# One decode step of attention beside a gated feed-forward: the first K tile's score products split around V's

## The chip, the cores and the metric

The kernel runs on one core of one Trainium2 chip. The metric is device time in microseconds of one execution; the kernel before took 2516.11 us, the median of 3 runs (2516.02 to 2516.18). The core has TensorE (PE, matrix products into the PSUM memory), VectorE (DVE), ScalarE (ACT), GpSimd (POOL) and SyncE (SP, which issues the transfers here). The engines run side by side and are tied to one another by semaphores.

## The reference

One token `x` of 512 values goes through two branches, and a gate mixes their outputs. Branch a is attention with 32 heads of 128 values against a cache of 65,536 keys and values for each head; branch b is a small gated feed-forward.

```python
q = (x @ wq).reshape(B, Sq, H, Dh).transpose(0, 2, 1, 3)
scores = einsum("bhqd,bhkd->bhqk", q, k_cache) * (Dh ** -0.5)
p = softmax(scores, axis=-1)
o = einsum("bhqk,bhkd->bhqd", p, v_cache)
a = o.transpose(0, 2, 1, 3).reshape(B, Sq, H * Dh) @ wo
b = (silu(x @ w_gate) * (x @ w_up)) @ w_down
g = sigmoid((x * gate_w).sum(-1, keepdims=True))
return g * a + (1 - g) * b
```

All inputs are bf16. The two caches are 537 MB each, nearly all of the 1087.65 MB that the kernel reads.

## The kernel before

*Tiles and buffers.* The keys of one head are cut into 4 tiles of 16,384 rows, which lie as 128 partitions x 128 keys x 128 values, and two tiles make a pair of 8.39 MB. There are 64 pairs (M), numbered m, two for each head. Two K buffers take the pairs in turn, and one V buffer holds a pair of V. They fill nearly all of the on-chip memory.

*Steps.* The first two pairs are handled in `prologue`. Then every engine runs steps m = 2, 3, ...: step m computes the scores of K pair m and applies the softmax weights of the head before to V pair m - 2. The 60 steps m = 2 to 61 are loops on VectorE, ScalarE and TensorE, with two steps to a round on TensorE; the last two are written out in `vector_end` and `tensor_end`. A head's first step is called b = 0 and its second b = 1 (`second` on TensorE).

*Scores.* VectorE multiplies a K tile by the query, repeated along the keys (`product`, L279), and then halves the 128 values by adding (L291, L309). Of the first tile of a pair only one halving is done (`add_once`, to 64 values, `WIDE`), then TensorE adds up the 64 in 16 products with the unit matrix into the bank `S_ps[0]`, 4 values each (`scores`, L513): the wide score products. The second tile is halved three times, the last time into `T_sb` with 16 values (`WIDTH`), and TensorE adds these in 4 narrow products into `S_ps[1]`. In either bank 4 values a key are left, which VectorE adds into `S_sb` (`fold`, L320). After a head's fourth tile VectorE takes the maximum (`row_max`, L326), which goes over ScalarE (`diag`) and TensorE (`max_turn`, L530) to `top_of` in the next step.

*V.* ScalarE turns a head's scores into weights `P_sb` (L417), half a head a step. TensorE then runs 64 products on V's pair (`values`, L537), each with 4 keys a partition as weights against 512 columns.

*Order on the engines.* Each engine runs its instructions in the order written. On TensorE a step has: in b = 1 the totals of the weights (`total`, L533); the 16 wide products; in b = 0 the wait for `P_sb`; the wait for V; V's 64 products; in b = 0 `total`; the query's spread for a later head (`query_spread`, L527); the 4 narrow products; the output's turn (`head_turn`, L545); `max_turn`. On VectorE: `product` of the first tile, `add_once`, `top_of` (b = 0) or the fold of the tile before (b = 1), `product` of the second tile, in b = 1 the three small instructions of `weight`, two sums, the fold of the first tile, the last sum into `T_sb`, and in b = 1 the second tile's fold and `row_max`.

*Loads.* SP issues all large loads into one queue, in the order V pair m - 1, K pair m + 2 (`sync_step`). The V load waits until V pair m - 2 is used up (`pe_V`, at the end of V's 64 products). The K load waits for the first narrow product of step m (`pe_K`), ahead of which every read of that K buffer stands. In `sync_end` the last tiles come singly, in halves or in smaller pieces, and then the output weights `wo`.

*Signals.* `take` waits for a credit and uses it up: `c_S[0]` comes from `add_once`, `c_S[1]` from the sum into `T_sb`, `c_P` from the weights, `c_V` from V's landing (through POOL), `c_q`, `c_o` and `c_m` from ScalarE. `fold` waits for `pe_S`, which the last of a tile's score products raises.

Of the kernel before, what the change touches and what calls it, by code (L numbers as in the profile page):

```python
# [11 lines left out]
NB = 128  # L12
PAIR = 2 * NB
QUAD = 4


WIDE = 64
WIDTH = 16

TURNED = 8  # L20
WO_CUTS = (0, 4, 8, 12, 16, 20, 24, 28, 30, 31, 32)
# [19 lines left out]
def kernel(  # L41
# [36 lines left out]
    def sb(name, shape, dtype=f32):  # L78
        return consts.tile(shape, dtype, name=name)
# [7 lines left out]

    T_sb = sb("T_sb", [P, NB, WIDTH], bf16)
    S_sb = [sb(f"S{i}_sb", [P, NBH]) for i in range(2)]
# [4 lines left out]
    ident_b, ones_b, q_diag = (sb(n, [P, P], bf16) for n in ("ident_b", "ones_b", "q_diag"))  # L94
# [16 lines left out]
    S_ps = [psum.tile([P, NB, QUAD], f32, name=f"S{i}_ps") for i in range(2)]  # L111
# [14 lines left out]
    def halves(buf):  # L126
        return [buf[:, i * NB * Dh : (i + 1) * NB * Dh].rearrange("p (j d) -> p j d", d=Dh) for i in range(2)]

    K_half, V_half = [halves(b) for b in K_bufs], halves(V_buf)
# [3 lines left out]
    def v_view(n):  # L133
        return {N - 4: K_half[0][1], N - 3: V_half[0], N - 2: V_half[1], N - 1: K_half[1][1]}[n]

    sync, act, dve, pool, pe = nc.sync, nc.scalar, nc.vector, nc.gpsimd, nc.tensor
# [3 lines left out]
    po, pe_x, pe_S, pe_V, pe_q, pe_m, pe_t, pe_o = (  # L140
        Events(nc, n) for n in ("po", "pe_x", "pe_S", "pe_V", "pe_q", "pe_m", "pe_t", "pe_o")
    )
# [24 lines left out]
    def wait(engine, events, value):  # L167
        key = id(engine), id(events)
        value -= taken.get(key, 0)
        if seen.get(key, 0) < value:  # L170
            engine.wait_ge(events.sem, value)
            seen[key] = value
# [88 lines left out]
    def product(n, start=0, stop=NB):  # L261
        K = K_half[n // 2 % 2][n % 2][:, start:stop, :]
        q = q_sb[n // G % 2]
        q_rep = bass.AP(tensor=q.tensor, offset=q[:, :].offset, ap=[list(q[:, :].ap[0]), [0, stop - start], [1, Dh]])
        m = n // 2

        if m == 0:
            wait(dve, (ka_in, kb_in)[n], 16)
        elif m == 1:
            wait(dve, kc_in, 16)  # L270
        elif n == N - 1:
            wait(dve, kb_in, 32)
        else:
            wait(dve, k_in[m % 2], 16 * (m // 2))
        if n < G:
            wait(dve, ac, marks["q"])
        else:
            wait(dve, ac_q, n // G)
        return own[0](dve.tensor_tensor(out=K, in0=K, in1=q_rep, op=ALU.mult))  # L279

    def add_halves(n, width, last, out=None, ahead=None):
        K = K_half[n // 2 % 2][n % 2]
        half, mark = Dh // 2, last
        while half >= width:
            wait(dve, own[0], mark)
            to = K[:, :, 0:half]
            if half == width and ahead is not None:
                fold(ahead)
            if half == width and out is not None:
                to = out  # L290
            ins = dve.tensor_tensor(out=to, in0=K[:, :, 0:half], in1=K[:, :, half : 2 * half], op=ALU.add)  # L291
            if half == width and out is not None:
                ins.then_inc(c_S[n % 2], 1)
            else:
                mark = own[0](ins)
            half //= 2
        marks["K", n] = mark
# [8 lines left out]
    def add_once(n, last):  # L306
        wait(dve, own[0], last)
        K, half = K_half[n // 2 % 2][n % 2], Dh // 2
        dve.tensor_tensor(  # L309
            out=K[:, :, 0:half], in0=K[:, :, 0:half], in1=K[:, :, half:], op=ALU.add  # L310
        ).then_inc(c_S[0], 1)


    def fold(n):
        h, g = divmod(n, G)
        if n < G or n >= N - G:
            wait(dve, pe_D, n + 1 if n < G else n + 1 - N + 2 * G)
        else:
            wait(dve, pe_S, n + 1 - G)
        return own[0](dve.tensor_reduce(  # L320
            out=S_sb[h % 2][:, g * NB : (g + 1) * NB], in_=S_ps[n % 2], axis=AXIS.X, op=ALU.add
        ))

    def row_max(h, folded):
        wait(dve, own[0], folded)
        (dv_max if h else dv_first)(dve.tensor_reduce(out=m_sb[:, 0:1], in_=S_sb[h % 2], axis=AXIS.X, op=ALU.max))  # L326

    def top_of(h):
        wait(dve, pe_m, 2 * h + 2)
        dv_top(dve.tensor_reduce(out=top[:, 0:1], in_=mT, axis=AXIS.X, op=ALU.max))  # L330

    def weight(h, t):
        wait(dve, pe_t, t)
        if h < H - 1:
            wait(dve, own[0], own[0](dve.tensor_reduce(out=tsum[:, 0:1], in_=tot, axis=AXIS.X, op=ALU.add)))
            total = tsum[:, 0:1]
        else:
            total = tot[:, 0:1]
        wait(dve, own[0], own[0](dve.reciprocal(recip[:, 0:1], total)))  # L339
        dv_rg(dve.tensor_tensor(out=rg[:, h % 2 : h % 2 + 1], in0=recip[:, 0:1], in1=gval, op=ALU.mult))  # L340

    def vector_step(m):
        h, b = divmod(m, MH)
        width, to = (WIDTH, T_sb) if m < M - 2 else (WIDE, None)
        last = product(2 * m)
        if to is not None:
            add_once(2 * m, last)
        if b == 0:
            top_of(h - 1)
        else:  # L350
            fold(2 * m - 1)
        if to is None:
            add_halves(2 * m, width, last)
        last = product(2 * m + 1)
        if b == 1:
            weight(h - 1, m - 1)
        add_halves(2 * m + 1, width, last, to, 2 * m)
        if b == 1:
            row_max(h, fold(2 * m + 1))

# [13 lines left out]
    def vector_round():  # L374
        own[0] = dv_loop
        for m in range(2, 2 + 2 * MH):
            vector_step(m)
        take_round(dve, dv_loop, vector_waits)
        own[0] = dv

    def vector_end():
        took_rounds(dve, vector_waits, (M - 4) // (2 * MH))
        vector_step(M - 2)
        vector_step(M - 1)
        top_of(H - 1)
        weight(H - 1, M - 1)
        wait(dve, pe_x, 5)
        out_a(dve.tensor_copy(out=out_sb[:, :HD], in_=a_ps[0]))
# [118 lines left out]
    def take(credit):  # L507
        pe.wait_ge(credit, 1)
        pe.sem_inc(credit, -1)  # L509

    def scores(n, src, width, events, start=0, stop=NB):
        for c in range(0, width, QUAD):
            ins = pe.matmul(  # L513
                S_ps[n % 2][:, start:stop, :], lhsT=ident_b, rhs=src[:, start:stop, c : c + QUAD],
                start=(c == 0), stop=(c == width - QUAD),
            )
            if c == 0 and events is pe_S and n == 1:
                pe_K(ins)
        if stop == NB:
            events(ins)  # L520

    def scores_direct(n, start=0, stop=NB):
        wait(pe, dv, marks["K", n])
        scores(n, K_half[n // 2 % 2][n % 2], WIDE, pe_D, start, stop)

    def query_spread(events):
        events(pe.matmul(qb, lhsT=ones_b, rhs=q_diag, start=True, stop=True))  # L527

    def max_turn(n=1):
        pe.matmul(mT, lhsT=ones_f, rhs=diag, start=True, stop=True).then_inc(pe_m.sem, n)  # L530

    def total(n=2):
        pe_t(pe.matmul(tot[:, :n], lhsT=ones_f, rhs=rs[:, :n], start=True, stop=True))  # L533

    def values(probs, view, start, stop, opens, closes):
        for j in range(start, stop, 4):
            ins = pe.matmul(  # L537
                O_ps, lhsT=probs[:, j : j + 4], rhs=view[:, j : j + 4, :],
                start=(opens and j == start), stop=(closes and j == stop - 4),
            )  # L540
        return ins

    def head_turn(opens=True):
        for c in range(4):
            ins = pe.matmul(  # L545
                oh, lhsT=O_sb[:, c * Dh : (c + 1) * Dh], rhs=ident_f[0:4, c : c + 1],
                start=(opens and c == 0), stop=(c == 3),
            )
        pe_o(ins)
# [133 lines left out]
    def tensor_step(m):  # L683
        second = m % MH
        if second:
            take(c_P)
            total()
        take(c_S[0])
        scores(0, K_half[m % 2][0], WIDE, pe_S)
        if not second:  # L690
            take(c_P)
        take(c_V)
        for i in range(2):
            pe_V(values(P_sb[:, i * NB :], V_half[i], 0, NB, i == 0, i == 1))
        if not second:
            total()
        take(c_q)
        query_spread(pe_q)
        take(c_S[1])
        scores(1, T_sb, WIDTH, pe_S)  # L700
        take(c_o)
        head_turn()
        take(c_m)
        max_turn()
# [115 lines left out]
```

## Time and profile before

| | us |
|---|---|
| unprofiled, median of 3 | 2516.11 |
| profiled execution, whole time | 2517.2 |
| its span | 2515.4 |
| VectorE busy in it | 2003.4 |
| TensorE busy (with modelled ends) | 1487.4 |
| ScalarE busy | 182.3 |

The three instructions of the loop that matter most: `product` of a tile is 8.7 us on VectorE (mean 8620 ns over 129, of which two are half tiles), a V product 379 ns from start to modelled end, a wide or tail score product 527 ns likewise. Matmuls overlap one another, so for their pace the spacing of their weight loads is read and not their duration.

How to read the lines below: a line of the timeline has its start, its length, the engine, the line of the kernel, the operation and out<-in, how many instructions were merged into it, and in brackets how long the engine stood idle before it and what ended that. SPq is SP issuing a load, PEld is TensorE loading weights. "PEclk" is the clock that TensorE was granted, as a share of full speed. The DMA share is the mean over the 16 transfer engines; in short windows it and the GB/s scatter, since a packet is counted where it ends.

### The profile page before, as it was taken

How to read it: one execution, taken by the hardware profiler on the slowest of the kernel's cores; microseconds unless marked ns; L12 is line 12 of the kernel's file. 1: busy time of each engine (PE TensorE's matmuls, PEld its weight loads, DVE VectorE, ACT ScalarE, POOL GpSimd, SP SyncE). 2: the span in 40 equal slices, each digit the busy share in tenths (PEclk: the TensorE clock that was granted, in tenths of full speed). 3: DMA queues.
4: the chain of work that ended last, by engine and by line, in shares of the span. 5: the costliest groups of instructions: out<-in, count | busy, mean ns of one | idle time of the engine just before them, and what ended most of it. 6: DMA issues, size and time to landing. Idle time of an engine off the chain costs nothing. (4 is left out here: it accounts for less than half of the span.)

```text
span 2515.4 us, 15705 instructions
## 1 busy us (share of the span) xinstructions
PE 1487.4 (59%) x6589; PEld 616.2 (24%) x6589; DVE 2003.4 (80%) x678; ACT 182.3 (7%) x503; POOL 0.7 (0%) x6
## 2 busy tenths in 40 slices
PE   2655655646556556465575565654745656547569
PEld 1322222222222222222222222222212222222223
DVE  5887887877878878779788788787787887977881
ACT  0000000000000000000000000000000000000000
POOL 0000000000000000000000000000000000000000
PEclk8777878778778777787787777877877778778789
DMA  9999999999999999999999999999999999999999
GB/s 414 438 433 436 435 434 434 434 434 434 435 434 434 434 434 434 435 436 435 435 435 434 437 434 435 435 434 437 435 434 434 434 434 434 434 435 434 434 431 387
DMA packets 22605, 1087.80 MB, mean 432 GB/s; under 512 B 2753, under 2 KB 3266, under 8 KB 4546
## 3 DMA queue, kind: packets, MB, share of 16 engines
q1 hardware_dynamic: 22306, 1087.65, 99.9%
q8 instruction: 7, 0.11, 0.0%
q10 hardware_dynamic: 288, 0.00, 0.0%
q14 instruction: 4, 0.03, 0.0%
HBM read 1087.64 MB, written 0.00 MB: 432 GB/s over the span
## 5 line engine op out<-in xcount | busy, mean ns | idle before, releaser
L279 DVE TENSOR_TENSOR K_buf<-K_buf,q_sb 128x16384 bf16<-128x16384 bf16 (+1 forms) x129 | 1112.0, 8620 | 348.8 <-DMA K_buf<-in_A_k_cache_dram 346.1
L513 PE MATMUL S_ps<-K_buf,ident_b 128*128 128x512 bf16 (+1 forms) x1104 | 388.9, 527 | 867.3 <-PEq L509 834.3
L537 PE MATMUL O_ps<-V_buf,P_sb 128*4 128x512 bf16 x3968 | 866.9, 379 | 28.6 <-PEq L509 28.3
L537 PEld LDWEIGHTS O_ps<-V_buf,P_sb 128*4 128x4 bf16 x3968 | 332.9, 85 | 560.1 <-issue 57.6
L291 DVE TENSOR_TENSOR K_buf<-K_buf 128x4096 bf16<-128x4096 bf16 (+1 forms) x127 | 433.7, 3415 | 3.1
L513 PEld LDWEIGHTS S_ps<-K_buf,ident_b 128*128 128x128 bf16 x1104 | 133.5, 126 | 1101.0 <-issue 1036.8
L309 DVE TENSOR_TENSOR K_buf<-K_buf 128x8192 bf16<-128x8192 bf16 x60 | 265.5, 4425 | 2.0
L392 ACT ACTIVATE O_sb<-O_ps 4x512 f32<-4x512 f32 x63 | 63.3, 1005 | 1705.1 <-PE qm_ps L527 1674.8
L320 DVE TENSOR_REDUCE S_sb<-S_ps 128x128 f32<-128x512 f32 x128 | 88.2, 689 | 105.4 <-PE S_ps L513 103.3
L530 PE MATMUL qm_ps<-diag,ones_f 128*128 128x128 f32 x126 | 33.5, 353 | 72.3 <-PEq L509 70.2
L545 PE MATMUL oh_ps<-ident_f,O_sb 4*128 4x1 f32 x504 | 64.3, 244 | 19.6 <-PEq L509 19.6
L291 DVE TENSOR_TENSOR T_sb<-K_buf 128x2048 bf16<-128x2048 bf16 x60 | 72.9, 1214 | 0.0
L545 PEld LDWEIGHTS oh_ps<-ident_f,O_sb 4*128 4x128 f32 x504 | 60.7, 186 | 49.7 <-issue 49.7
L513 PE MATMUL S_ps<-T_sb,ident_b 128*128 128x512 bf16 x240 | 64.7, 391 | 0.0
L530 PEld LDWEIGHTS qm_ps<-diag,ones_f 128*128 128x128 f32 x126 | 21.6, 215 | 76.3 <-issue 76.3
L392 ACT ACTIVATE bias<-top 128x1 f32<-128x1 f32 x32 | 6.5, 203 | 436.4 <-DVE top L330 436.4
L533 PE MATMUL tot_ps<-rs,ones_f 128*128 128x2 f32 (+1 forms) x126 | 24.8, 266 | 17.6 <-PEq L509 17.5
L392 ACT ACTIVATE oT<-whole_o,rg 32x1 f32 (+1 forms) x115 | 33.8, 294 | 4.7
L417 ACT ACTIVATE P_sb<-S_sb,bias 128x256 bf16<-128x256 f32 x62 | 31.5, 508 | 1.0
L533 PEld LDWEIGHTS tot_ps<-rs,ones_f 128*128 128x128 f32 x126 | 20.3, 202 | 36.5 <-issue 36.5
L513 PEld LDWEIGHTS S_ps<-T_sb,ident_b 128*128 128x128 bf16 x240 | 20.7, 96 | 15.9
L326 DVE TENSOR_REDUCE m<-S_sb 128x1 f32<-128x512 f32 x32 | 22.0, 686 | 1.1
(62 smaller groups left out, 197.1 us busy)
## 6 DMA issues: line engine op xcount, KB each, us to landing
K_buf<-in_A_k_cache_dram SPq DMA_DIRECT2D x4, 4096.0 KB, 32.9
V_buf<-in_A_v_cache_dram SPq DMA_DIRECT2D x2, 4096.0 KB, 21.3
V_buf<-in_A_v_cache_dram SPq DMA_DIRECT2D x4, 2048.0 KB, 17.6
V_buf<-in_A_wq_dram SPq DMA_DIRECT2D x1, 4096.0 KB, 12.3
K_buf<-in_A_v_cache_dram SPq DMA_DIRECT2D x1, 4096.0 KB, 29.9
K_buf<-in_A_wo_dram SPq DMA_DIRECT2D x7, 512.0 KB, 16.8
K_buf<-in_A_v_cache_dram SPq DMA_DIRECT2D x3, 1024.0 KB, 23.5
V_buf<-in_B_w_gate_dram SPq DMA_DIRECT2D x1, 1792.0 KB, 54.4
```

Source lines behind the costliest of these rows:

```text
L279: return own[0](dve.tensor_tensor(out=K, in0=K, in1=q_rep, op=ALU.mult))
L291: ins = dve.tensor_tensor(out=to, in0=K[:, :, 0:half], in1=K[:, :, half : 2 * half], op=ALU.add)
L309: dve.tensor_tensor(out=K[:, :, 0:half], in0=K[:, :, 0:half], in1=K[:, :, half:], op=ALU.add).then_inc(c_S[0], 1)
L320: return own[0](dve.tensor_reduce(out=S_sb[h % 2][:, g * NB : (g + 1) * NB], in_=S_ps[n % 2], axis=AXIS.X, op=ALU.add))
L326: (dv_max if h else dv_first)(dve.tensor_reduce(out=m_sb[:, 0:1], in_=S_sb[h % 2], axis=AXIS.X, op=ALU.max))
L392: return act.activation(out=out, in_=in_, func=ACT.Copy, scale=scale)
L417: return act.activation(out=out, in_=S_sb[h % 2][:, b * PAIR : b * PAIR + count], func=ACT.Exp, bias=bias[:, 0:1], scale=scale, accum_out= ...
L513: ins = pe.matmul(S_ps[n % 2][:, start:stop, :], lhsT=ident_b, rhs=src[:, start:stop, c : c + QUAD], start=(c == 0), stop=(c == width - QUAD),
L530: pe.matmul(mT, lhsT=ones_f, rhs=diag, start=True, stop=True).then_inc(pe_m.sem, n)
L533: pe_t(pe.matmul(tot[:, :n], lhsT=ones_f, rhs=rs[:, :n], start=True, stop=True))
L537: ins = pe.matmul(O_ps, lhsT=probs[:, j : j + 4], rhs=view[:, j : j + 4, :], start=(opens and j == start), stop=(closes and j == stop - 4),)
L545: ins = pe.matmul(oh, lhsT=O_sb[:, c * Dh : (c + 1) * Dh], rhs=ident_f[0:4, c : c + 1], start=(opens and c == 0), stop=(c == 3),)
```

## The change

TensorE: of the 16 wide products of a step, the first 12 (48 of 64 values) stay ahead of V's products, and the other 4 come behind them. The bank `S_ps[0]` stays open in between, and `pe_S` for that tile is raised by the last of the four. VectorE: the fold of the first tile, which stood ahead of the second tile's last sum, stands behind it. This holds in all of `vector_step`, also for the two last steps, whose TensorE part (`tensor_end`) is not split. Nothing is added or taken away; the instructions on ScalarE, POOL and SP and their order are the same.

```diff
+AHEAD = 48
...
-    def add_halves(n, width, last, out=None, ahead=None):
+    def add_halves(n, width, last, out=None):
...
             to = K[:, :, 0:half]
-            if half == width and ahead is not None:
-                fold(ahead)
             if half == width and out is not None:
                 to = out
...
-        add_halves(2 * m + 1, width, last, to, 2 * m)
+        add_halves(2 * m + 1, width, last, to)
+        fold(2 * m)
         if b == 1:
             row_max(h, fold(2 * m + 1))
...
-    def scores(n, src, width, events, start=0, stop=NB):
-        for c in range(0, width, QUAD):
+    def scores(n, src, width, events, start=0, stop=NB, ahead=0):
+        for c in range(ahead, width, QUAD):
...
         take(c_S[0])
-        scores(0, K_half[m % 2][0], WIDE, pe_S)
+        K = K_half[m % 2][0]
+        for c in range(0, AHEAD, QUAD):
+            pe.matmul(S_ps[0], lhsT=ident_b, rhs=K[:, :, c : c + QUAD], start=(c == 0), stop=False)
         if not second:
             take(c_P)
         take(c_V)
         for i in range(2):
             pe_V(values(P_sb[:, i * NB :], V_half[i], 0, NB, i == 0, i == 1))
+        scores(0, K, WIDE, pe_S, ahead=AHEAD)
         if not second:
             total()
```

## The prediction

> **What bounds the kernel now.** I read the page's queue table first, then rates by long stretches, then the timeline of two steps of the loop, then the end.
>
> ```profile
> q1 hardware_dynamic: 22306, 1087.65, 99.9%
> HBM read 1087.64 MB, written 0.00 MB: 432 GB/s over the span
> ```
>
> One queue carries everything, and its packets fill 99.9% of the span of all 16 engines. The stretches (length, busy time of PE, PEld, DVE, ACT, POOL, then granted clock, DMA share, GB/s) show that this is a constant pace and no mean:
>
> ```profile
> 679.60:1066.00 386.40, 226.36 (x972) 92.99 (x971) 314.99 (x106) 29.26 (x80) 0.00 (x0) 0.77 1.00 434
> 1066.00:1452.40 386.40, 227.38 (x972) 92.91 (x971) 314.99 (x106) 29.24 (x80) 0.00 (x0) 0.77 1.00 434
> 1452.40:1838.90 386.50, 226.18 (x972) 92.78 (x971) 315.06 (x106) 29.24 (x80) 0.00 (x0) 0.76 1.00 434
> ```
>
> VectorE, the busiest engine, works 315 of 386 us: it has room. Now the timeline over two steps, thinned to what hands on buffers; the bracket is idle time of that engine before the line:
>
> ```profile
> 1046.72 0.33 SPq L181 DMA_DIRECT2D V_buf<-in_A_v_cache_dram  x1
> 1047.34 0.33 SPq L181 DMA_DIRECT2D K_buf<-in_A_k_cache_dram  x1
> ...
> 1051.87 8.69 DVE L279 TENSOR_TENSOR K_buf<-K_buf,q_sb 128x16384 bf16<-128x16384 bf16 x1 [8.10 <-DMA K_buf<-in_A_k_cache_dram]
> ...
> 1065.16 6.24 PE L513 MATMUL S_ps<-K_buf,ident_b 128*128 128x512 bf16 x16 [14.39 <-PEq L509]
> ...
> 1070.24 0.14 PEld L513 LDWEIGHTS S_ps<-K_buf,ident_b 128*128 128x128 bf16 x1 [0.28 <-issue]
> 1070.59 0.31 PEld L513 LDWEIGHTS S_ps<-K_buf,ident_b 128*128 128x128 bf16 x2 [0.21 <-issue]
> ...
> 1071.33 13.97 PE L537 MATMUL O_ps<-V_buf,P_sb 128*4 128x512 bf16 x64
> ...
> 1081.38 0.69 DVE L320 TENSOR_REDUCE S_sb<-S_ps 128x128 f32<-128x512 f32 x1
> 1081.98 1.21 DVE L291 TENSOR_TENSOR T_sb<-K_buf 128x2048 bf16<-128x2048 bf16 x1
> ...
> 1085.31 1.08 PE L513 MATMUL S_ps<-T_sb,ident_b 128*128 128x512 bf16 x4
> 1085.34 0.33 SPq L181 DMA_DIRECT2D V_buf<-in_A_v_cache_dram  x1
> 1085.73 0.41 SPq L181 DMA_DIRECT2D K_buf<-in_A_k_cache_dram  x1
> ...
> 1086.42 0.69 DVE L320 TENSOR_REDUCE S_sb<-S_ps 128x128 f32<-128x512 f32 x1 [3.22 <-PE S_ps L513]
> 1087.15 0.69 DVE L326 TENSOR_REDUCE m<-S_sb 128x1 f32<-128x512 f32 x1
> ...
> 1090.46 8.69 DVE L279 TENSOR_TENSOR K_buf<-K_buf,q_sb 128x16384 bf16<-128x16384 bf16 x1 [2.63 <-DMA K_buf<-in_A_k_cache_dram]
> ```
>
> Each step moves one K pair and one V pair, 16.78 MB. K lands at 1051.87 and 1090.46, 38.6 us apart, so each of the two takes 19.3 us and V lands near 1071.2. V's buffer is free, and its next load issued, at 1085.34, while the K load ahead of it in the queue still runs for 1090.46 - 1085.34 = 5.1 us. That 5.1 us is the cover: the queue has work when the next load is put behind it. At the start of the kernel the first load is issued at 0.96 and the first 5 us move at 223 GB/s, or 1.12 MB, 2.6 us' worth at 434; so data began to flow about 1.5 us after the issue. I count the cover as 5.1 - 1.5 = 3.6 us. A step's work on the chip costs time only by what it is late beyond that.
>
> **The change, part by part.** A score product of the wide tile takes 0.427 us while the granted clock reads 0.5 (spacing of the weight loads: 0.14 + 0.28) and about 0.22 once it reads 1.00; V's 64 take 13.97, or 0.218 each.
>
> *Four products behind V.* Before, all 16 run from 1065.16 to 1071.3 and V's begin at 1071.33, about when V lands; in the other step of a head they begin at 1026.48, and V's begin at 1032.71 after a gap of 1.1 us. Twelve need 12 x 0.427 = 5.1 us at the slow clock, to 1070.3. V's start can therefore come no more than 0.1 us earlier (it lands near 1071.2), and not at all in the step with the gap. I take 0, bounds 0 and 0.1 us a step. V's release, and with it the next V load, stays at 1085.3.
>
> *What stands behind the four.* After V they run warm: 4 x 0.22 = 0.9 us. PE's queue behind them holds the totals, the query's spread, the 4 products of the narrow tile, the head's turn and the maximum's turn; all come 0.9 us later. The first narrow product releases K's buffer, so K's load is issued at 1086.6 instead of 1085.73. It stands behind a V load of 19.3 us: cost 0; without that V load ahead it would cost 0.9. ScalarE's copies of the output and the next exponentials, at 1049.47 in the first step, come 0.9 later and are wanted at 1065: cost 0.
>
> *The fold moved.* VectorE's last sum comes 0.6 us earlier, which only moves T_sb's readiness from 1083.2 to 1082.6, while its reader on PE is held behind V until 1085.3: gain 0. The fold then waits for the last of the 16, at 1085.3 + 0.9 = 1086.2, and ends at 1086.9. Behind it on VectorE stand the second fold (its products end near 1087.2, it ends at 1088.0) and the row maximum, to 1088.7 against 1087.8 before. The next product waits for K until 1090.46, so VectorE's idle time of 2.63 shrinks to 1.8: cost 0. In the other step only the one fold follows, to 1048.3, against 1051.87. Where a lateness beyond 1.8 us arose, the next K product, its 12 score products and V's start would follow, with 0.9 us more of slack ahead of V and the 3.6 us cover behind.
>
> *The same edit in the last two steps.* There the last sum is on the listed chain, and 0.6 us comes off ahead of the last tiles' scores. What it triggers is loads:
>
> ```profile
> 2456.00:2460.00 4.00, 4.00 (x21) 1.55 (x19) 4.00 (x3) 0.00 (x0) 0.00 (x0) 1.00 1.00 434
> 2460.00:2464.00 4.00, 3.48 (x17) 1.41 (x16) 1.04 (x1) 0.00 (x0) 0.00 (x0) 1.00 1.01 434
> ```
>
> The queue is full there too. Counted back from the last landing at 2510.7 in 9.66 us per 4.19 MB (the output weights, then tiles 127, 126, 125), tile 125's data begin at 2472.1, and its load was issued at 2460.61: 11.5 us early. So 0.6 us off costs and gives 0; if the queue ran dry there it would give 0.6.
>
> *Unknown: an accumulation left open.* The first score bank stays open while V's 64 go to another bank, and PE changes tile twice more. No row shows that. The nearest is each change from scores to V, with 0.42 us of idle weight load before it: bounds 0 and 2 x 0.42 = 0.8 us a step, inside the cover of 3.6. I take 0.
>
> *Unknown: the clock in the gap.* PE now stands idle 1 to 2 us between its 12 and V. The granted clock falls to 0.5 in each step's long idle stretch, and the longest half-clock stretch of busy products is 2447.09 to 2452.98, 5.9 us. If such a stretch fell wholly on V, 5.9/0.427 = 14 products would lose 0.21 us each: 2.9 us, inside 3.6. Bounds 0 and 2.9 us late, cost 0 either way. The Trainium skill, "TensorE: Matmul & The Clock Gate", section "What's actually happening", says the clock halves after an idle window of about 3.4 us and returns after a busy one of that length, on windows that run free. By it the gap of 1 to 2 us alone would seldom slow V, and then for one window, 1.7 us as an estimate; the sum would still be 0.
>
> **Sum.** 0 on the profiled execution, whose span is 2515.4 and whose whole time is 2517.2, 1.1 above the unprofiled median of 2516.11. Forecast: 2516.1.
>
> **The rivals.** *Slower: V's products run cold.* Place: the start of V in every step. It decides once more than 3.6/0.21 = 17 of V's products are at half clock, a stretch of 7.3 us; each step then leaves the queue dry. At 9 us it is 21 products, 4.4 us, 0.8 beyond the cover, and over 60 steps 48 us: 2564. For it: the gap is new, and idle PE does lose its clock. Against: no half-clock stretch of busy products is over 5.9 us, and lateness closes the gap that causes it.
>
> *Faster: PE sets the pace, and the full queue only shows loads waiting on it.* In the 30 steps where V's start follows the scores without a gap, four products ahead of it go, at 0.22 to 0.427 each, so 0.9 to 1.7 us: 26 to 51 us, middle 2478. Against: VectorE waits for K's landing in both kinds of step (8.10 and 2.63), which it would not if loads were early. If 434 GB/s is the limit, little can be had at all: the loop's rate over 59 steps (V loads at 119.12 and 2399.24, 38.65 us a step) is 434.1, and 1087.65 MB at that is 2505.4; 2.4 us are lost at the start and 4.7 after the last landing, so 2.9 are left, and the floor is 2513.2. The Trainium skill, "DMA: Bandwidth & Descriptors", section "Where 436 GB/s comes from", puts a ceiling of 435 GB/s on the 16 engines; by it the floor stands and this rival falls.
>
> *The change doesn't do what it says:* V starts no earlier, since it starts on landing. By my rows that is nearly so, and the time is the same 2516.1.
>
> **How the numbers follow.** Loads set the pace: 0.80, of which V starting no earlier at all is 0.5. Cold V: 0.14, since no row shows V behind a gap as long as the new one. PE's pace: 0.06. I call 0.2%, 5 us, what a measurement of this kernel can tell from no change. The floor of 2513.2 lies within it, so faster is only PE's pace, 0.06; slower is cold V, 0.14; same is 0.80. The range's low end is that floor, 2513. Its high end allows five odd steps with the 0.8 us above: 2520. Cold V and PE's pace lie outside, with 0.20.
>
> **What would show it.** In the profile after: 434 GB/s in the long stretches, 38.6 us between V loads, and 5 us from V's issue to K's next landing; VectorE's wait for K at a head's second step near 1.8 us, that at the first near 3.6, with a new wait of some 3.6 us on PE ahead of the moved fold; K's load some 1.3 us after V's. It is wrong if V's 64 take much over 14 us, if the share of DMA falls under 1.00 in any stretch of the loop, or if the rate itself moves.

## The result: slower by 0.27%, and the profile after

The changed kernel takes 2522.9 us (median of 9 runs, 2519.69 to 2528.12) against 2516.45 for the kernel before (9 runs, 2516.02 to 2517.5). The ratio is 1.0027, with a 95% interval of 1.0018 to 1.0035. Two things are new: the time, which lies outside the range of 2513 to 2520, and the spread, 8.4 us instead of 1.5.

In the profiled execution of after (2525.6 us, span 2523.8, so 8.4 above the span before) the queue moves the same 22,306 packets, a little more slowly:

```profile
q1 hardware_dynamic: 22306, 1087.65, 99.8%
...
HBM read 1087.64 MB, written 0.00 MB: 431 GB/s over the span
```

The loss is not spread evenly. These are stretches of four steps each and the last steps of the loop (columns as in the prediction: busy times of the engines, then clock, DMA share, GB/s), first of after:

```profile
1840.70:1995.30 154.60, 91.49 (x390) 37.51 (x389) 126.41 (x43) 11.71 (x32) 0.00 (x0) 0.76 1.00 435
1995.30:2149.90 154.60, 91.76 (x384) 37.06 (x381) 123.84 (x41) 11.72 (x32) 0.00 (x0) 0.76 1.00 429
2149.90:2304.50 154.60, 95.62 (x388) 37.92 (x388) 121.54 (x42) 11.23 (x32) 0.00 (x0) 0.76 0.99 421
2304.50:2400.00 95.50, 57.14 (x238) 22.92 (x239) 81.16 (x29) 3.98 (x13) 0.00 (x0) 0.76 1.00 432
```

and one such stretch of before:

```profile
2149.90:2304.50 154.60, 91.27 (x389) 37.17 (x388) 126.03 (x43) 11.23 (x32) 0.00 (x0) 0.76 1.00 434
```

The third stretch moves 421 instead of 434 GB/s, which is 154.6 x 13/434 = 4.6 us; the second loses 1.8 us in the same way (154.6 x 5/434). Most steps lose nothing. What is special there stands in the timeline of after, two steps of that third stretch:

```profile
2150.17 4.04 PE L692 MATMUL S_ps<-K_buf,ident_b 128*128 128x512 bf16 x12 [13.73 <-PEq L510]
...
2156.35 15.58 PE L538 MATMUL O_ps<-V_buf,P_sb 128*4 128x512 bf16 x64 [2.14 <-PEq L510]
...
2158.87 0.13 PEld L538 LDWEIGHTS O_ps<-V_buf,P_sb 128*4 128x4 bf16 x1 [0.30 <-issue]
2159.30 0.13 PEld L538 LDWEIGHTS O_ps<-V_buf,P_sb 128*4 128x4 bf16 x1 [0.30 <-issue]
2159.68 11.74 PEld L538 LDWEIGHTS O_ps<-V_buf,P_sb 128*4 128x4 bf16 x55 [0.26 <-issue]
...
2171.97 0.33 SPq L183 DMA_DIRECT2D V_buf<-in_A_v_cache_dram  x1
...
2173.22 0.33 SPq L183 DMA_DIRECT2D K_buf<-in_A_k_cache_dram  x1
...
2175.50 8.69 DVE L281 TENSOR_TENSOR K_buf<-K_buf,q_sb 128x16384 bf16<-128x16384 bf16 x1 [0.17 <-DMA K_buf<-in_A_k_cache_dram]
...
2196.91 15.66 PE L538 MATMUL O_ps<-V_buf,P_sb 128*4 128x512 bf16 x64 [2.91 <-PEq L510]
...
2212.60 0.33 SPq L183 DMA_DIRECT2D V_buf<-in_A_v_cache_dram  x1
...
2216.09 8.69 DVE L281 TENSOR_TENSOR K_buf<-K_buf,q_sb 128x16384 bf16<-128x16384 bf16 x1 [1.82 <-DMA K_buf<-in_A_k_cache_dram]
```

PE idles 2.14 us between its 12 products and V's, and then V's 64 take 15.58 us instead of 13.97: the first eight run 0.43 us apart (0.13 + 0.30), and from 2159.7 on the usual pace is back. The next V load goes out 3.5 us before K lands (2171.97 to 2175.50), where the kernel before had 5.1. K's next landing is at 2216.09, 40.6 us after the last, 2.0 more than a step's 38.6. V's products that begin at 2196.91 take 15.66 again, and their load goes out at 2212.60, 3.5 us ahead of K.

A step of after that loses nothing has a gap of 0.94 us and V at full pace:

```profile
1071.91 13.97 PE L538 MATMUL O_ps<-V_buf,P_sb 128*4 128x512 bf16 x64 [0.94 <-PEq L510]
...
1085.92 0.33 SPq L183 DMA_DIRECT2D V_buf<-in_A_v_cache_dram  x1
```

V's 64 products of a step are called a V run here, a cold one where part of it ran at half clock. Counted over the 60 steps of the loop, after has 9 cold V runs of 15.6 us, each with 3.3 to 3.4 us at half clock. The gaps ahead of these are 2.02 to 2.91 us. The other 51 take 13.97 us with gaps up to 1.94. Before has none, and no gap over 1.31.

The granted clock (PEclk) shows the drop. First four windows of after around V's start at 2156.35, then three around a gap of 1.94 us that did no harm:

```profile
2149.39:2152.81 3.42, 2.64 (x7) 1.01 (x8) 3.42 (x3) 0.00 (x0) 0.00 (x0) 0.50 0.97 422
2152.81:2156.22 3.41, 1.40 (x7) 0.41 (x5) 3.41 (x1) 0.00 (x0) 0.00 (x0) 1.00 0.84 365
2156.22:2159.64 3.42, 3.29 (x8) 1.00 (x9) 3.35 (x5) 0.00 (x0) 0.00 (x0) 0.50 1.24 537
2159.64:2163.05 3.41, 3.41 (x17) 1.36 (x16) 3.41 (x2) 0.00 (x0) 0.00 (x0) 1.00 0.81 348
...
1258.51:1261.93 3.42, 3.04 (x8) 1.10 (x9) 3.42 (x3) 0.81 (x3) 0.00 (x0) 0.50 1.28 556
1261.93:1265.34 3.41, 1.48 (x8) 0.51 (x7) 3.41 (x1) 0.00 (x0) 0.00 (x0) 1.00 0.76 327
1265.34:1268.75 3.41, 3.41 (x18) 1.31 (x17) 3.38 (x2) 0.00 (x0) 0.00 (x0) 1.00 1.37 596
```

These windows aren't chosen freely. In the clock records of every trace here, all changes of the clock within one execution lie on a fixed grid of 3.413 us. In all nine cold steps of after the clock had risen before V began and fell again at a grid point from 0.1 us before to 1.0 us after V's start. The grid window up to that point, with the gap in it, had PE busy for 41% of its length or less (1.40 of 3.41 us above). Where PE was busy for 43% or more of a window with the gap in it (1.48 us), the clock stayed. So what counts is how much of one grid window the gap takes up.

What the queue does after a late V load, in windows of 2 us of after (a packet counts whole in the window in which it starts):

```profile
2212.00:2214.00 2.00, 2.00 (x12) 0.93 (x11) 0.42 (x1) 0.23 (x1) 0.00 (x0) 1.00 1.06 360
2214.00:2216.00 2.00, 1.67 (x11) 1.06 (x9) 0.27 (x1) 0.83 (x1) 0.00 (x0) 1.00 0.50 197
2216.00:2218.00 2.00, 0.81 (x4) 0.59 (x4) 1.91 (x1) 0.99 (x4) 0.00 (x0) 0.92 1.16 492
```

Right behind the load issued at 2212.60 the DMA share falls to 0.50. Such windows scatter in any step, but the records of single packets agree: 0.75 us after that issue only 5 of the 16 engines had a packet under way, where in the steady part all 16 have one all the time.

The same count parts the nine cold steps. Behind the V loads at 1048.92, 1164.88 and 1898.89 all 16 engines had a packet all the time, and the next K landed 38.6 us after the last, as ever. Behind the other six at least one engine had none for a while, and the next K landed 0.7 to 2.0 us late.

### The profile page after: what moved, and what is told of

Its sections match the earlier page's. It is cut to its first block, busy times and chain, and to the rows that moved or that the text cites. A ratio compares the mean times of both kernels' runs of the same rounds, so it can differ in the third digit from the quotient of the medians.

```text
span 2523.8 us, 15644 instructions
## 1 busy us (share of the span) xinstructions
PE 1495.9 (59%) x6589; PEld 616.5 (24%) x6589; DVE 2009.1 (80%) x678; ACT 182.6 (7%) x503; POOL 0.7 (0%) x6
## 3 DMA queue, kind: packets, MB, share of 16 engines
q1 hardware_dynamic: 22306, 1087.65, 99.8%
## 5 line engine op out<-in xcount | busy, mean ns | idle before, releaser
L538 PE MATMUL O_ps<-V_buf,P_sb 128*4 128x512 bf16 x3968 | 881.8, 383 | 88.0 <-PEq L510 88.0
L692 PE MATMUL S_ps<-K_buf,ident_b 128*128 128x512 bf16 x720 | 291.0, 584 | 773.9 <-PEq L510 773.9
L692 PEld LDWEIGHTS S_ps<-K_buf,ident_b 128*128 128x128 bf16 x720 | 91.8, 133 | 943.0 <-issue 937.5
L514 PE MATMUL S_ps<-K_buf,ident_b 128*128 128x512 bf16 (+1 forms) x384 | 103.6, 407 | 34.0 <-DVE K_buf L291 26.4
L514 PEld LDWEIGHTS S_ps<-K_buf,ident_b 128*128 128x128 bf16 x384 | 34.1, 103 | 98.2 <-issue 43.0
```

Source lines behind the costliest of these rows:

```text
L514: ins = pe.matmul(S_ps[n % 2][:, start:stop, :], lhsT=ident_b, rhs=src[:, start:stop, c : c + QUAD], start=(c == 0), stop=(c == width - QUAD),
L538: ins = pe.matmul(O_ps, lhsT=probs[:, j : j + 4], rhs=view[:, j : j + 4, :], start=(opens and j == start), stop=(closes and j == stop - 4),)
L692: pe.matmul(S_ps[0], lhsT=ident_b, rhs=K[:, :, c : c + QUAD], start=(c == 0), stop=False)
```

## The experiments

The gap theory: the change leaves PE idle ahead of V; where that gap is long enough, the clock drops for a window, V ends 1.6 us late, its buffer's next load is issued 1.6 us late, and the transfer engines run dry. It has rivals at each link: that the moved fold holds VectorE, that the work now behind V comes too late, that a V load so little late can't matter, that a cold V run costs PE or VectorE directly. Ratios are to the kernel before.

| run | us | ratio, 95% interval | cold V runs of 60 | longest gap, us |
|---|---|---|---|---|
| fold_only | 2516.28 | 0.9999 (0.9990 to 1.0008) | 0 | 1.3 |
| filled_gap | 2516.72 | 1.0001 (0.9992 to 1.0010) | 0 | 1.2 |
| filled_32 | 2516.72 | 1.0001 (0.9992 to 1.0010) | 0 | 1.2 |
| ahead_56 | 2516.42 | 1.0000 (0.9991 to 1.0009) | 0 | 1.8 |
| after | 2522.9 | 1.0027 (1.0018 to 1.0035) | 9 | 2.9 |
| ahead_44 | 2537.6 | 1.0090 (1.0067 to 1.0113) | 28 | 3.7 |
| ahead_32 | 2547.48 | 1.0129 (1.0113 to 1.0145) | 55 | 4.8 |

The last two columns are counted in each profiled execution, and the time is the median of all runs; a V run is called cold over 14.2 us.

**The fold alone (fold_only).** From after:

```diff
-        K = K_half[m % 2][0]
-        for c in range(0, AHEAD, QUAD):
-            pe.matmul(S_ps[0], lhsT=ident_b, rhs=K[:, :, c : c + QUAD], start=(c == 0), stop=False)
+        scores(0, K_half[m % 2][0], WIDE, pe_S)
...
-        scores(0, K, WIDE, pe_S, ahead=AHEAD)
```

> All 16 wide products ahead of V as before; only VectorE's fold stays behind the last sum. Gap theory (PE's idle gap ahead of V lets its clock drop for one window, V ends 1.6 us late, the next V load is issued too late): the gap is that of before (at most 1.31 us), no V run of 64 over 14.0 us, time 2516 to 2517. Fold rival (the moved fold holds VectorE and makes the next K product late): as after, 2520 or more.

It is at the time of before. The fold's new place alone costs nothing; the loss needs the split on PE.

**The gap filled (filled_gap, filled_32).** From after, and the same with 8 in place of 4 and AHEAD = 32:

```diff
             pe.matmul(S_ps[0], lhsT=ident_b, rhs=K[:, :, c : c + QUAD], start=(c == 0), stop=False)
+        for i in range(4):
+            pe.matmul(O_ps, lhsT=ident_b[:, 0:4], rhs=K[:, 4 * i : 4 * i + 4, :], start=True, stop=True)
```

> As after, but 4 more products, whose result is not used (they write the output bank before V's products overwrite it), stand between the 12 score products and V: the gap is filled, the 4 score products behind V and the moved fold stay. Gap theory: no V run of 64 over 14.0 us, time 2516 to 2517. Rival of the later work (the 4 products behind V make K's load, the folds and the maximum late): as after, 2520 or more.

> As ahead_32, with 8 more products whose result is not used filling the gap between the 8 score products and V. Gap theory: all of ahead_32's loss goes, no V run over 14.0 us, 2516 to 2517.5, although 8 products still stand behind V. Rival of the later work: the loss of ahead_32 stays in part, 2520 or more.

Both are back at the time of before, though 4 and 8 products still stand behind V. The useless products close the gap, but they also make the burst ahead of V longer; that the gap is what slows V in after is read from its clock, which had risen before V began in all nine. The timeline of filled_gap:

```profile
1026.68 4.13 PE L692 MATMUL S_ps<-K_buf,ident_b 128*128 128x512 bf16 x12 [12.22 <-PEq L510]
...
1030.75 1.02 PE L694 MATMUL O_ps<-K_buf,ident_b 128*4 128x512 bf16 x4
1032.93 13.97 PE L538 MATMUL O_ps<-V_buf,P_sb 128*4 128x512 bf16 x64 [1.15 <-PEq L510]
...
1046.93 0.33 SPq L183 DMA_DIRECT2D V_buf<-in_A_v_cache_dram  x1
...
1048.32 0.33 SPq L183 DMA_DIRECT2D K_buf<-in_A_k_cache_dram  x1
...
1052.07 8.69 DVE L281 TENSOR_TENSOR K_buf<-K_buf,q_sb 128x16384 bf16<-128x16384 bf16 x1 [3.48 <-DMA K_buf<-in_A_k_cache_dram]
```

Four products without use shorten the gap to 1.15 us, V takes 13.97, and V's load has its 5.1 us again, while K's load still goes out 1.4 us after it. Nor does VectorE's new wait matter. The waits of filled_gap (time, times, longest) are those of a kernel that lost nothing:

```profile
DVE S_sb L320 <- PE S_ps L514: 261.1, 92, 4.7
DVE K_buf L281 <- DMA K_buf<-in_A_k_cache_dram: 184.7, 64, 22.9
```

Against 103.3 and 346.1 before, the fold's wait has merely taken the place of a wait for K.

**The split at other places (ahead_56, ahead_44, ahead_32).** `AHEAD = 56`, 44 and 32 in after: 14, 11 and 8 products ahead of V.

> 14 products ahead of V, 2 behind. In after, every V run whose gap was 2.02 us or more ran slow, none at 1.94 or less. Two products more ahead cut the gap by 0.4 us, to at most 1.75. Gap theory: no V run over 14.0 us, 2516 to 2517. A loss in proportion to the number moved (the rival of the later work) gives half of after's 6 us: about 2519.

> 11 products ahead, 5 behind: the gap grows by 0.2 to 0.4 us to 1.1 to 2.4. Gap theory: 15 to 25 V runs of 15.6 us in place of 9, 2521 to 2540. A loss in proportion to the number moved: 5/4 of after's 6 us, 2524, with as few slow V runs as after; the count of V runs tells the two apart, the time alone does not.

> 8 products ahead of V and 8 behind. Gap theory: the gap grows by some 1 to 1.7 us to 2.0 to 4, nearly all 60 V runs take 15.6 us, and at about 0.9 us lost for each (8.4 us over 9 of them in after) the time is 2550 to 2575. Rival of the later work: K's load and the folds come 0.9 us later than in after, which loses at most about twice its 8 us: 2525 to 2535, with V runs of 14.0 us.

With 14 ahead nothing is lost, with 11 ahead 21 us, three times after's 6.5 for a quarter more products moved. So the loss is no price per product; it comes with the count of cold V runs, 0, 9, 28, 55. The count for 11 came out above what was expected (28, not 15 to 25) and the time for 8 just under it (2547.5, not 2550 or more). In the profiled execution of ahead_32 (span 2541.4) a cold V run costs 26.0/55 = 0.5 us, against 8.4/9 = 0.9 in after.

With fewer products ahead there is a second way to a cold V run, which the gap theory didn't have. In 6 of the 28 in ahead_44 and 28 of the 55 in ahead_32 the clock didn't drop in the gap: it had not yet risen when V began. One is the V run of ahead_44 at 690.42, behind a gap of 1.30 us:

```profile
686.77:690.18 3.41, 2.35 (x6) 0.58 (x4) 3.41 (x1) 0.00 (x0) 0.00 (x0) 0.50 0.84 365
690.18:693.60 3.42, 3.18 (x8) 1.00 (x9) 3.37 (x3) 0.00 (x0) 0.00 (x0) 0.50 1.15 498
```

There the shorter burst, and not the gap alone, leaves V cold.

**The V load alone made late (late_v_load, late_v_small).** From before; PE and VectorE keep their order:

```diff
-            wait(sync, pe_V, 2 * i)
+            wait(sync, pe_W, i)
             load_pair(V_buf, A_v_cache, i, vA_in)
...
+            if c == 0:
+                pe_W(ins)
         pe_o(ins)
```

`pe_W` is raised by the first product of the output's turn; in late_v_small by the second narrow product. SP issues K's next load behind V's, so that comes later too, but it has V's 19.3 us of transfers ahead of it.

> The kernel before, with PE and VectorE untouched; the V load alone waits for the first product of the output's turn instead of the last product of V, so it is issued 1.6 to 1.9 us later in every step of the loop. If the cover of 3.6 us in the prediction were right: 2516 to 2517. Gap theory (a V load 1.6 us late is enough to cost): 2525 to 2575, between 0.15 and 1 us a step.

> The kernel before, with the V load alone waiting for the second narrow product: some 0.6 us later in each step (late_v_load: 1.9 us later, 1.2 us lost a step). If the first of the 16 engines to finish K sets the cover and 1 us or so is left over: 2516 to 2518. If there is no cover beyond what before uses, each 0.6 us is lost: up to 2516 + 60 x 0.6 = 2552.

late_v_load took 2588.39 us, ratio 1.0277 (1.0259 to 1.0294), with only 2 cold V runs. The loss is in the queue, four steps of late_v_load:

```profile
1000.00:1154.60 154.60, 88.26 (x369) 35.51 (x370) 125.99 (x42) 9.79 (x28) 0.00 (x0) 0.76 1.00 423
```

It loses 72 us over the 60 loads that were moved, 1.2 us each, for a lateness of 1.4 to 2.0 (median 1.75). late_v_small took 2519.24 (2517.23 to 2523.61), ratio 1.0011 (1.0002 to 1.0020): 0.6 to 0.85 us of lateness costs 2.9 us in all. In its profiled execution, the slowest of the 11, seven steps lose 0.4 to 3.1 us each, and the others next to nothing. Behind the V load an engine had no packet under way in 5 of 60 steps of before, in 19 of late_v_small and in 57 of late_v_load. So the cover begins to give out near 0.6 us and is gone at 1.75. The trace's records of each engine's landing, which no view prints, say why. Time from the V load's issue until an engine had landed its last piece of the K load ahead of it, us:

```
                               first   median   last of the 16
before (median of 60 loads)     3.30     3.88     5.12
after, load at 2171.97          1.45     1.83     3.51
after, load at 2212.60          0.53     0.89     3.47
late_v_small (median)           2.91     3.70     4.30
late_v_load (median)            1.26     1.81     3.39
```

VectorE's product starts when the last engine has landed, so the 5.1 us read from it is the last engine's. The first ends 1.8 us earlier, and each engine runs dry for itself. A load doesn't start at once either: the first packets of the 16 engines began 2.10 to 3.07 us into before, 1.1 to 2.1 after the first issue at 0.96. As an estimate from these rows, the cover is 3.3 less 1.1 to 2.1, so 1.2 to 2.2 us in a median step and less in some.

**V loaded in halves (after_v_halves, ahead_32_v_halves, before_v_halves).** This gives the load room and leaves PE alone:

```diff
-        if i < M - 3:
-            wait(sync, pe_V, 2 * i)
-            load_pair(V_buf, A_v_cache, i, vA_in)
-        else:
-            for n in (2 * i, 2 * i + 1):
-                wait(sync, pe_V, n - 1)
-                load_tile(V_half[n % 2], A_v_cache, n, (vA_in, vB_in)[n % 2])
+        for n in (2 * i, 2 * i + 1):
+            wait(sync, pe_V, n - 1)
+            load_tile(V_half[n % 2], A_v_cache, n, (vA_in, vB_in)[n % 2])
```

and `tell_of_v` waits for both halves.

> As after, but each V pair is loaded in two halves, the first issued when the first half of V's 64 products is done, some 7 us earlier than now. The clock and the gap are left as they are. Gap theory: the slow V runs stay (5 to 15 of them at 15.6 us), but a V load 1.6 us late is no longer too late, so the time is 2515 to 2517.5. Rival (a slow V run costs time on PE or VectorE itself, whatever the queue holds): 2520 or more.

> As ahead_32 (2547), with V loaded in two halves. Gap theory: 50 or more slow V runs, and 2515 to 2519, since the queue never waits for V's release. Rival (PE or VectorE itself): most of the 31 us stays, 2535 or more.

> The kernel before with V loaded in two halves. If the transfers alone set its pace: 2515.5 to 2517, within 0.1% of before. If before itself loses something to a short cover: down to the floor of 2513. If loads in runs half as long (32 KB a partition) move more slowly: over 2518.

The three take 2518.65, 2518.65 and 2518.67 us, ratios 1.0008, 1.0008 (both 0.9999 to 1.0017) and 1.0009 (1.0000 to 1.0018), with 5, 52 and 0 cold V runs. The group of V's products in ahead_32_v_halves (busy time, mean ns of one, idle before):

```profile
L536 PE MATMUL O_ps<-V_buf,P_sb 128*4 128x512 bf16 x3968 | 959.5, 407 | 126.1 <-PEq L508 126.1
```

In before that group is busy for 866.9 us at 379 ns. The cold V runs are all there, 92.6 us more of busy time, and cost nothing: a cold V run costs time through its late load alone. All three lie 2.4 us above before, the same with any split: ahead_32_v_halves inside what was expected, after_v_halves 1.2 us above, and before_v_halves in its last case, loads half as long that move a little more slowly. The 59 steps of its loop from K's landing to K's landing take 38.69 us on average in place of 38.65; whether the shorter pieces or the second issue do that was not told apart. So this version repairs the loss but doesn't beat the kernel before. No version tried did.

## Why the prediction was wrong

*What held.* Transfers set the pace, and no work was added to their path. The moved fold costs 0 (fold_only). The 4 products behind V cost 0, K's load came 1.25 to 1.40 us after V's, where some 1.3 was forecast. In steps whose V ran at full pace VectorE's wait for K is 1.76 us at a head's second step and 3.53 at its first, forecast 1.8 and 3.6, and the moved fold's wait for PE is 3.71 and 4.46, forecast some 3.6. Two of the signs that it named for being wrong came: V's 64 products at 15.6 us and a DMA share of 0.99 in a stretch of the loop. The change of tile on PE with the accumulation left open costs 0 (filled_gap has it too).

*The step that failed* is the cover: "I count the cover as 5.1 - 1.5 = 3.6 us." It took the last engine's landing for the queue's. Measured, 0.6 to 0.85 us of lateness already costs 2.9 us over the kernel, the 1.6 to 1.7 us of a cold V run cost something in 6 of 9 steps, and 1.4 to 2.0 cost 1.2 us a step: the cover is some 0.6 to 1.7 us, step by step, and not 3.6. Every later sentence that set a lateness against 3.6 fell with it: "2.9 us, inside 3.6 ... cost 0 either way".

*The rival "V's products run cold" was the right mechanism*, with its place (the start of V) and its cause (the new gap). Its point of decision was mis-sized by the same step: it was put at 17 products at half clock, 7.3 us, and one window of 3.4 us with 8 such products was enough. Hence also the price: not 48 us from 60 steps, but 6.5 in the median run; the profiled execution lost 8.4, in 6 of its 9 cold steps. "Lateness closes the gap that causes it" was half right: cold V runs come one to three in a row, but the 2.91 us gap behind a late load shows that lateness can open the gap too, since V then lands late as well.

*The Trainium skill*, "TensorE: Matmul & The Clock Gate", section "What's actually happening", gave the size of a drop in the prediction: one window, 1.7 us. The traces agree on that (3.3 to 3.4 us at half clock, 1.6 to 1.7 us lost) and on windows that don't follow the work (the grid of 3.413 us). On when the clock drops they differ: no wholly idle window was needed, one in which PE was busy for up to 41% was enough, so gaps from 2.02 us on. The prediction made "seldom" of the rule; it was 9 times in 60.

*A reading that was off beside it.* The prediction gave the gap of 1.1 us ahead of V to one of a head's two steps. In the loop of before the gap goes in threes and not in twos (1.12, 0, 0.52, 0.97, 0 from 1032.71 to 1187.30), as three steps of 38.65 us are 33.97 grid windows. This touched only the price of its faster rival.

*Open.* Why the next K comes up to 2.0 us late where an engine was without a packet for less: behind the V load at 2014.89 one or two of the 16 had none for 0.7 us in all, and 1.5 us were lost. And the spread of after from run to run: the grid of the clock lies elsewhere against the kernel's start in each trace (first change at 43.37 us in after, 43.10 in before), so it can meet the gap otherwise in each run. That would give the spread, but there is one trace of after, so it is only argued.

## What to carry to other kernels

Before work is moved out of a wait, look at what the engine does in that wait: on TensorE an idle gap of some 2 us ahead of the critical products can slow them, where it falls inside one window of the clock's grid, and so can too short a burst ahead of them. Useless products in the gap can be worth their place. The time until a transfer lands, read from the engine that waits for it, is the last transfer engine's time; the next load must be issued for the first one, so measure the cover by making the load late on purpose before you call a lateness free. A queue that is 99.9% full says nothing of how near it is to running dry.

## What the hardware showed that was not expected

- The clock changed only on a grid of 3.413 us in each of the 13 traces. Over all V runs, the 76 drops at V's start followed a grid window with PE busy for at most 42.6%; the lowest share that kept the clock was 41.6%. Gaps of 2.02 us and more did it in after, and none up to 1.94.
- So the gap alone doesn't decide. In ahead_44 four V runs were cold after gaps of 1.30 to 1.47 us because the clock had not risen yet. In late_v_load a gap of 3.09 us (V's start at 1181.97) went without a drop: it lay across a grid point, and the two windows had PE busy for 62 and 47%.
- The 16 engines finish one load up to 1.8 us apart (3.30 to 5.12 us after the issue of the next, median over before).
- Two V loads of 32 KB for each partition in place of one of 64 KB cost 2.4 us in 2516, about 0.1%.
